# Softmax sums over partitions by accumulating DMAs, values of all groups kept in DRAM, five probability tiles

## The chip, the cores and the metric

The kernel runs on one core of a Trainium2 chip. The metric is the device time of one execution in microseconds. Of each kernel there are several timed runs, whose median counts, and one execution taken with the hardware profiler, whose records are called the trace here. Engines are named as the profile names them: PE is TensorE (matmuls), PEld its weight loads, DVE is VectorE, ACT is ScalarE, POOL is GpSimd, and SP is SyncE, which issues nearly all DMAs. A name such as L364 is line 364 of the kernel before.

## The reference

One input `x` of 2048 tokens by 1024 is normalised and goes two ways.

```
xn  = layernorm(x)
# A: attention, 32 heads of 32
q, k, v = split(xn @ wqkv)
p   = softmax(q @ k.T / sqrt(32), axis=keys)
s   = concat_heads(p @ v) @ wo
# B: a router picks 8 tokens, they go through a SwiGLU FFN (F = 3584) and are added back
r   = xn @ w_r ; idx = top 8 of r
y   = (silu(xn[idx] @ w_gate) * (xn[idx] @ w_up)) @ w_down * sigmoid(r[idx])
g   = silu(xn + scatter(y, idx))
out = x + s * g
```

The change concerns the softmax: each query's exponentials have to be summed over all 2048 keys, and the attention output is divided by that sum. All of it is float32 in and out.

## The kernel before

**Tiling.** The 32 heads are worked on in 8 groups `g` of 4 heads (`NG = 8`, the last is `L = 7`). In a group the 2048 queries are 4 blocks `qb` of 512, and the 2048 keys are 16 tiles `kt` of 128. One step of the main loop is a unit `(g, qb, kt)`; there are 512 units, 16 to a block, 32 blocks in all. Scores are computed with keys on the partitions: for a unit, `scores` makes 4 heads x 128 keys x 512 queries on PE in two halves, and ACT takes the exponential of each half into a probability tile `pt` of 128 x 2048 float32 (L357). No maximum is subtracted. `values` multiplies the tile with the values of its 128 keys (L371) and accumulates over the 16 units in one PSUM bank `oa`.

**The sums.** The denominators need the sum over all keys, thus over units and over partitions. Over units, DVE adds every tile into the tile of `kt = 0` of the block, which is the accumulator (`add`, L364: 15 adds a block). Over partitions, `sums` multiplies the accumulator with a matrix of ones on PE (L389, eight instructions for four heads because float32 takes two each), ACT copies the result (`ds`, L391), and SP writes 4 x 512 numbers to DRAM (`d_d`, L396) and reads them back spread over 128 partitions (`dr`, L397). `reciprocals` takes 1/x on DVE, SP writes it to DRAM and reads it back broadcast to all rows (`rb`, L414), `normalise` multiplies the block's output with it (L420), and `split_o` splits the product in two float16 parts, which SP stores (L429).

**Buffers.** There are four `pt` tiles: one is the accumulator, three rotate. A tile is free again when its add and its value matmuls are done; the accumulator is free after `sums`. Tiles of one tag are given out in the order in which they were freed. `v` has 16 tiles, `hl` two, `o32` (the block's unnormalised output) one.

**Projections.** Beside the units PE computes the next group's Q, K and V (`chain`, `pair_v`, `chain_v`). V is computed for two groups at once for groups 1 to 6 (`pair_v`): the first of the pair goes straight to SBUF, the second to DRAM (`v_d`), from which `load_v` fetches it a group later. Groups 0 and 7 are computed alone (`chain_v`) straight into SBUF.

**Order.** The order on PE, DVE, ACT and SP is written out by hand: a loop runs over the units, and in unit `u` issues `scores(u + 1, 0)`, one item of the filling work, `scores(u + 1, 1)`, `add(u)`, `values(u)`, then what is due in that unit (`side`, filled by `on` and `at`), then more filling work according to its planned cost. A function that returns another one has that one issued a unit later (`go`, `soon`). In each unit's turn of the before kernel, the block before is finished at fixed places:

```python
        if block:
            for at, h in ((1, sums), (5, reciprocals), (9, normalise), (10 if before[0] == L else 11, split_o)):
                if kt == at:
                    go(lambda: h(*before))
```

Every queue works strictly in this order; SP too, so that a DMA that waits for its data holds back all DMAs behind it. GpSimd is not in the hand-written order; it has the router's index work and one gather in group 2, and 16 gathers of the routed rows in the last group. In groups 1 to 3 DVE also runs the router's dot products (`route_dot`), and in blocks 17 to 28 SP fetches the FFN's weights in slices of 448 KB, 96 of them.

## Time and profile before

| | us |
|---|---|
| median of 3 runs | 1687.06 (1686.96 to 1687.82) |
| the profiled execution | 1685.43 |
| span of the profiled execution | 1683.6 |
| PE busy in it | 1651.3 |
| DVE busy | 1420.2 |
| ACT busy | 1195.8 |
| GpSimd busy | 48.0 |
| mean granted TensorE clock | 0.998 |

The span is the time from the first to the last instruction of the program in the trace. A row of a group of instructions reads: line, engine, operation, output<-input, shapes, count | busy us, mean ns of one | idle us of the engine just before them, and what ended it. Matmuls overlap in the array: busy time is the union of their spans, and the time that a group takes from the others is seen from its start to the next group's start. A row of a timeline reads: start us, duration us, engine, line, operation, tiles, count. DMA rows on `SPq` show when SP issued them, not when the data landed. In a stretch's row stand its length, the busy time of each engine with the number of instructions, the granted clock, the DMA engines' busy share and GB/s.

### The profile page before, as it was taken

The page shows a single profiled execution, that of the slowest core. Times are in us where ns is not written, and L with a number is a line of the kernel's source. Part 1 is how long each engine was busy: PE and PEld are TensorE (multiplying, and loading weights), DVE is VectorE, ACT ScalarE, POOL GpSimd, SP SyncE. Part 2 cuts the span into 40 slices and gives each one's busy share as a digit, 9 for nine tenths or more (in the row PEclk, how much of TensorE's full clock was granted, in tenths as well). Part 3 has the DMA queues.
Part 4 walks back from the last instruction along what each step waited for, and adds up shares of the span by engine and source line. Part 5 has one row for each costly group of instructions (what it writes and reads, how often), then busy time and mean ns, then how long its engine had stood idle before and what let it go on. Part 6 is the DMA issues. An engine that isn't in the chain of part 4 may idle for free.

```text
span 1683.6 us, 60567 instructions
## 1 busy us (share of the span) xinstructions
PE 1651.3 (98%) x27809; PEld 951.6 (57%) x27809; DVE 1420.2 (84%) x1122; ACT 1195.8 (71%) x1366; POOL 48.0 (3%) x41
## 2 busy tenths in 40 slices
PE   6999999999999999999999999999999999999998
PEld 5756877756565445455556554444444444455666
DVE  8687788989999989989988888888887989887862
ACT  5666777777787778778777777777777777765530
POOL 0000000000000000000000000000000002021110
PEclk9999999999999999999999999999999999999999
DMA  6222223222332222222334345345434455443442
GB/s 244 82 62 85 68 65 100 66 72 85 109 99 69 68 87 94 74 81 73 95 113 133 114 144 151 104 131 162 132 108 146 120 158 162 133 141 118 158 168 91
DMA packets 129985, 187.98 MB, mean 112 GB/s; under 512 B 21731, under 2 KB 91667, under 8 KB 129467
## 3 DMA queue, kind: packets, MB, share of 16 engines
q1 hardware_dynamic: 127370, 183.86, 35.2%
q8 instruction: 219, 3.59, 0.9%
q0 software_dynamic: 2352, 0.17, 0.1%
q14 instruction: 44, 0.35, 0.1%
HBM read 151.92 MB, written 40.41 MB: 114 GB/s over the span
## 4 chain that ended last, share of the span: by engine, by line
PE 83%; DVE 9%; ACT 3%; issue 3%; DMA 2%; SPq 0%; DVEq 0%; ACTq 0%
PE sc L236 22%; PE oa L371 22%; PE proj L236 16%; PE wop L236 10%; DVE pt L364 6%; PE vp L236 5%; PE vp L276 2%; ACT pt L357 2%; PE dn L389 2%; PE proj L256 2%; PE ffn L565 1%; PE py L596 1%; PE xtp L192 1%; DVE w L226 0%; DVE hl L325 0%
## 5 line engine op out<-in xcount | busy, mean ns | idle before, releaser
L357 ACT ACTIVATE pt<-sc 128x1024 f32<-128x1024 f32 x1024 | 997.4, 1024 | 358.4 <-PE sc L236 274.5
L364 DVE TENSOR_TENSOR pt<-pt 128x2048 f32<-128x2048 f32 x480 | 1097.0, 2288 | 98.1 <-ACT pt L357 80.1
L236 PE MATMUL sc<-qs,ks 96*32 96x512 f16 x8192 | 639.5, 379 | 10.1 <-ACT pt L357 10.0
L371 PE MATMUL oa<-pt,v 128*32 128x512 f32 x4096 | 543.2, 592 | 0.0
L236 PE MATMUL proj<-xt,w 128*32 128x512 f16 x5664 | 428.1, 379 | 0.0
L236 PEld LDWEIGHTS <-ks 96*32 96x32 f16 x8192 | 260.5, 97 | 166.1 <-issue 39.1
L236 PEld LDWEIGHTS <-w 128*32 128x32 f16 x5664 | 184.8, 96 | 216.3 <-issue 138.1
L371 PEld LDWEIGHTS oa<-pt,v 128*32 128x32 f32 x4096 | 149.4, 110 | 80.4 <-ACT o L382 2.8
L236 PEld LDWEIGHTS <-xt 128*32 128x32 f16 x4608 | 145.0, 96 | 80.8 <-issue 64.8
L236 PE MATMUL vp<-w,xt 128*32 128x256 f16 x4608 | 178.2, 272 | 0.0
L236 PE MATMUL wop<-wo,ot 128*32 128x512 f16 (+1 forms) x3168 | 173.5, 373 | 0.5 <-DVE z L708 0.5
L236 PEld LDWEIGHTS <-ot 128*32 128x32 f16 x3168 | 111.2, 97 | 70.8 <-issue 22.0
L325 DVE SCALAR_TENSOR_TENSOR hl<-proj,hl 128x512 f16<-128x512 f32 x64 | 44.1, 689 | 65.8 <-ACT hl L324 65.7
L708 DVE SCALAR_TENSOR_TENSOR z<-wop,z 128x512 f32<-128x512 f32 (+1 forms) x33 | 22.2, 675 | 62.8 <-PE wop L236 62.7
L276 PEld LDWEIGHTS <-xt 128*128 128x128 f16 x768 | 45.5, 100 | 7.7 <-issue 7.2
L276 PE MATMUL vp<-w,xt 128*128 128x128 f16 x768 | 49.2, 223 | 0.0
L324 ACT ACTIVATE hl<-proj 128x512 f16<-128x512 f32 x64 | 38.2, 597 | 14.6 <-PE proj L236 10.6
L565 PEld LDWEIGHTS ffn<-wf,xst 128*32 128x32 f32 x512 | 17.1, 108 | 38.0 <-issue 35.7
L226 DVE SCALAR_TENSOR_TENSOR w<-wraw,w 128x1024 f16<-128x1024 f32 x24 | 29.3, 1220 | 9.1 <-ACT w L221 9.1
L565 PE MATMUL ffn<-wf,xst 128*32 128x224 f32 x512 | 36.3, 352 | 0.0
L192 PE MATMUL xtp<-ident,xin 128*128 128x128 f32 x128 | 19.4, 302 | 15.0 <-DVE xin L183 7.8
L391 ACT ACTIVATE ds<-dn 128x512 f32<-128x512 f32 x32 | 19.2, 599 | 21.1 <-PE dn L389 20.9
(130 smaller groups left out, 636.5 us busy)
## 6 DMA issues: line engine op xcount, KB each, us to landing
st<-hl SPq DMA_DIRECT2D x64, 256.0 KB
wf<-in_B_w_gate_dram SPq DMA_DIRECT2D x32, 448.0 KB
wf<-in_B_w_up_dram SPq DMA_DIRECT2D x32, 448.0 KB
wd<-in_B_w_down_dram SPq DMA_DIRECT2D x32, 448.0 KB
wraw<-in_A_wqkv_dram SPq DMA_DIRECT2D x24, 512.0 KB
ks<-st SPq DMA_DIRECT2D x96, 128.0 KB
qs<-st SPq DMA_DIRECT2D x96, 128.0 KB
xr<-in_A_x_dram SPq DMA_DIRECT2D x16, 512.0 KB
```

Source lines behind the costliest of these rows:

```text
L192: nc.tensor.transpose(XP[t][:, k, :], xn[:, k * P:(k + 1) * P], ident)
L226: nc.vector.scalar_tensor_tensor(hl[:, 1], WR[c, g], WS, hl[:, 0], op0=ALU.mult, op1=ALU.subtract)
L236: nc.tensor.matmul(out[c], w[:, c], x, **flags)
L256: (nc.tensor.matmul if hold is not None else narrow)(box["ps"][:, cols], w[:, wi, k, :], xt[:, xi, k, cols], start=(n == 0), stop=(n == 23))
L276: nc.tensor.matmul(box["ps"][:, tt, :], xt[:, xi, k, t % 4 * P:(t % 4 + 1) * P], w[:, wi, k, :], start=(k + wi + xi == 0), stop=(k + wi == ...
L324: nc.scalar.activation(hl[:, 0], ps, AF.Copy, scale=KQ)
L325: nc.vector.scalar_tensor_tensor(hl[:, 1], ps, KQ, hl[:, 0], op0=ALU.mult, op1=ALU.subtract)
L357: nc.scalar.activation(PT[u][:, 2 * hf:2 * hf + 2], ps, AF.Exp, bias=0.0, scale=ESC)
L364: nc.vector.tensor_add(ACC[g, qb], ACC[g, qb], PT[u])
L371: nc.tensor.matmul(OA[g, qb][32 * j:32 * j + 32, :], VT[g, kt // 2][:, kt % 2, 32 * j:32 * j + 32], PT[u][:, j, :], start=(kt == 0), stop= ...
L389: nc.tensor.matmul(dn[32 * j:32 * j + 32, :], ones, acc[:, j, :], start=True, stop=True)
L565: nc.tensor.matmul(box[i][32 * j:32 * j + 32, :], RT["xst"][:, k, :], wt[:, j * FQ:(j + 1) * FQ], start=(k == 0), stop=(k == KT - 1))
```

## The change

For groups 0 to 6 (28 of the 32 blocks) the sum over partitions no longer goes through PE. `fold` writes the whole accumulator (1 MB) to DRAM from SP, and three DMAs issued by GpSimd add the upper half of its rows to the lower half: rows 64 to 127 onto 0 to 63, then 32, then 16. `fold_load` reads the 16 rows that are left back into SBUF, spread over the partitions (`dr16`), and `fold_rows` adds the 16 on DVE and goes on with the reciprocals as before. The places in the next block move from units 1, 5, 9 and 11 to 1 (`fold`), 9 (`fold_load`), 12 (`fold_rows`), 17 (`normalise`) and 18 (`split_o`); 17 and 18 are units 1 and 2 of the block after. The blocks of the last group keep the matmul with ones and units 1, 5, 9 and 10.

There are five `pt` tiles in place of four and two `o32` in place of one. `v` goes from 16 tiles to 10: the values of groups 1 to 7 are all stored to DRAM, a pair in one copy of ACT and one store, and fetched one by one as the group before ends. Value tiles on their way to DRAM and `ds` share the two `hl` buffers; `dr16` and a router tile share the buffer of `rb`.

```diff
+PTB = 5
...
-    v_d = dram.tile([NG // 2, NT // 2, P, 2, P], F32, name="v_d")
+    v_d = dram.tile([NG // 2, NT // 2, P, 2, 2, P], F32, name="v_d")
...
-    SLOTS = [("pt", 4)] * 8 + [("ks", KSB)] * 4 + [("qs", 2)] * 1 + [("big", 3)] * 1 + [("pt", 4)] * 2
+    SLOTS = [("pt", PTB)] * 8 + [("ks", KSB)] * 4 + [("qs", 2)] * 1 + [("big", 3)] * 1 + [("pt", PTB)] * 2
...
         def out():
-            nc.scalar.activation(v_tile(g, h), box["ps"], AF.Copy, scale=VS)
+            if g == 0:
+                nc.scalar.activation(v_tile(g, h), box["ps"], AF.Copy, scale=VS)
+                return
+            v = sb.tile([P, 2, P], F32, name="vs1", tag="hl", bufs=2)
+            nc.scalar.activation(v, box["ps"], AF.Copy, scale=VS)
+            return lambda: nc.sync.dma_start(v_d[(g - 1) // 2, h, :, :, 0], v)
...
-        VT[g, h] = v = sb.tile([P, 2, P], F32, name="v", tag="v", bufs=16)
+        VT[g, h] = v = sb.tile([P, 2, P], F32, name="v", tag="v", bufs=10)
...
         def out():
-            nc.scalar.activation(v_tile(g, h), box["ps"][:, :, 0], AF.Copy, scale=VS)
-            v = sb.tile([P, 2, P], F32, name="v", tag="v", bufs=16)
-            nc.scalar.activation(v, box["ps"][:, :, 1], AF.Copy, scale=VS)
-            return lambda: nc.sync.dma_start(v_d[g // 2, h], v)
+            v = sb.tile([P, 2, 2, P], F32, name="vs2", tag="hl", bufs=2)
+            nc.scalar.activation(v, box["ps"], AF.Copy, scale=VS)
+            return lambda: nc.sync.dma_start(v_d[(g - 1) // 2, h], v)
...
     def load_v(g, h):
-        nc.sync.dma_start(v_tile(g, h), v_d[(g - 1) // 2, h])
+        nc.sync.dma_start(v_tile(g, h), v_d[(g - 1) // 2, h, :, :, (g - 1) % 2])
...
-            PT[u] = sb.tile([P, 4, 512], F32, name="pt", tag="pt", bufs=4)
+            PT[u] = sb.tile([P, 4, 512], F32, name="pt", tag="pt", bufs=PTB)
...
-        o = sb.tile([P, 512], F32, name="o32", tag="o32", bufs=1)
+        o = sb.tile([P, 512], F32, name="o32", tag="o32", bufs=2)
...
-        ds = sb.tile([P, 512], F32, name="ds", tag="f512", bufs=1)
+        ds = sb.tile([P, 512], F32, name="ds", tag="hl", bufs=2)
...
+    def fold(g, qb):
+        a_d = dram.tile([P, 4 * 512], F32, name="a_d", tag="a_d", bufs=2)
+        nc.sync.dma_start(a_d, ACC.pop((g, qb)).rearrange("p j q -> p (j q)"))
+        for n in (64, 32, 16):
+            nc.gpsimd.dma_start(a_d[0:n], a_d[n:2 * n], accum_op=ALU.add, max_dma_last_dim=4096)
+        DN[g, qb] = a_d
+
+    def fold_load(g, qb):
+        a_d = DN[g, qb]
+        dr = DN[g, qb] = sb.tile([P, 16, 16], F32, name="dr16", tag="rb", bufs=1)
+        nc.sync.dma_start(dr, a_d[0:16].rearrange("r (p q) -> p r q", q=16))
+
+    def fold_rows(g, qb):
+        dr = small.tile([P, 2, 16], F32, name="dr", tag="dr")
+        nc.vector.tensor_reduce(dr[:, 0], DN[g, qb].rearrange("p r q -> p q r"), axis=AX.X, op=ALU.add)
+        DN[g, qb] = dr
+        return reciprocals(g, qb)
...
-        rt = sb.tile([NT, P], F32, name="rt", tag="f512", bufs=1)
+        rt = sb.tile([NT, P], F32, name="rt", tag="rb", bufs=1)
...
-            if qb == 3 and n > 1 and n % 2 == 0:
-                for h in range(7):
-                    on(g, qb, 2 * h + 3, load_v, n, h)
-                on(n, 0, 1, load_v, n, 7)
+            if qb == 3:
+                for h in range(6):
+                    on(g, qb, max(2 * h - 1, h), load_v, n, h)
+                for h in range(6, 8):
+                    on(n, 0, 2 * h - 8, load_v, n, h)
...
+    for b in range(NG * NB):
+        g, qb = divmod(b, NB)
+        for k, f in (((1, sums), (5, reciprocals), (9, normalise), (10, split_o)) if g == L else
+                     ((1, fold), (9, fold_load), (12, fold_rows), (17, normalise), (18, split_o))):
+            if b < NG * NB - 1:
+                at((b + 1) * NT + k, f, g, qb)
...
-        if block:
-            for at, h in ((1, sums), (5, reciprocals), (9, normalise), (10 if before[0] == L else 11, split_o)):
-                if kt == at:
-                    go(lambda: h(*before))
```

More of the change, by code (lines that the diff above doesn't have):

```diff
@@ L925, in _fast @@
         g, qb, kt = u
-        block = g * NB + qb
-        before = divmod(block - 1, NB)
         if kt == 0:
@@ L965, in _fast @@
             sides = sides[1:]
-        for at, h in ((2, sums), (12, reciprocals), (24, normalise), (26, split_o)):
-            if n == at:
+        for k, h in ((2, sums), (12, reciprocals), (24, normalise), (26, split_o)):
+            if n == k:
                 go(lambda: h(L, NB - 1))
```

## The prediction

> **What bounds the kernel now.** I read the page first (shares, then the chain that ended last), then busy times over single blocks, then the groups of instructions, then the timeline around one block's end. A block is 16 units of one query block; the stretches below are cut where a block's first `oa` matmul starts.
>
> ```profile
> PE 1651.3 (98%) x27809; PEld 951.6 (57%) x27809; DVE 1420.2 (84%) x1122; ACT 1195.8 (71%) x1366; POOL 48.0 (3%) x41
> ...
> PE 83%; DVE 9%; ACT 3%; issue 3%; DMA 2%; SPq 0%; DVEq 0%; ACTq 0%
> ```
> ```profile
> core 0: us, PE busy (x) PEld busy (x) DVE busy (x) ACT busy (x) POOL busy (x), PEclk, DMA share, GB/s
> ...
> 459.60:503.79 44.19, 44.19 (x781) 30.36 (x776) 41.21 (x29) 34.42 (x41) 0.00 (x0) 1.00 0.32 98
> 503.79:550.60 46.81, 45.00 (x785) 24.23 (x779) 43.49 (x48) 35.07 (x41) 1.20 (x1) 1.00 0.23 70
> 550.60:599.01 48.41, 45.56 (x789) 23.17 (x785) 46.78 (x44) 35.74 (x41) 0.00 (x0) 1.00 0.24 77
> ...
> 643.22:688.55 45.33, 44.67 (x781) 22.35 (x773) 44.36 (x30) 36.50 (x42) 0.00 (x0) 1.00 0.29 92
> ```
> ```profile
> 1054.89:1100.54 45.65, 45.65 (x702) 21.19 (x698) 39.80 (x25) 34.02 (x39) 0.00 (x0) 1.00 0.45 123
> ```
>
> In an ordinary block TensorE has no gap (44.19 busy of 44.19, so 44.19/16 = 2.76 us a unit) and the granted clock is 1.00. VectorE is second with 41.21, which leaves it 2.98 us. Three blocks of groups 2 and 3 are longer than 44.19, by 2.6, 4.2 and 1.1 us, and there VectorE fills 93 to 98% of the time. So TensorE work that disappears shortens nearly every block, until VectorE's 3 us are used up.
>
> **The removed sums.** Of 32 `dn` groups 28 go.
>
> ```profile
> 418.43 1.08 PE L371 MATMUL oa<-pt,v 128*32 128x512 f32 x8
> ...
> 419.29 1.07 PE L389 MATMUL dn<-pt,ones 128*32 128x512 f32 x8
> ...
> 420.15 0.65 PE L236 MATMUL proj<-xt,w 128*32 128x512 f16 x8
> ```
> ```profile
> L389 PE MATMUL dn<-pt,ones 128*32 128x512 f32 x256 | 33.9, 592 | 0.0
> ...
> L391 ACT ACTIVATE ds<-dn 128x512 f32<-128x512 f32 x32 | 19.2, 599 | 21.1 <-PE dn L389 20.9
> ...
> L312 ACT ACTIVATE v<-vp 128x256 f32<-128x256 f32 x24 | 9.4, 390 | 0.0
> ...
> L229 DVE TENSOR_REDUCE am<-wraw 128x1 f32<-128x1024 f32 x24 | 28.9, 1211 | 0.0
> ...
> L517 DVE TENSOR_REDUCE tf<-eq 128x16 f32<-128x128 f32 x1 | 0.3, 286 | 0.0
> ```
>
> The matmuls overlap, so the 33.9 us of busy time overstates them. From one group's start to the next group's start is 420.15 - 419.29 = 0.86 us, and the group before it is 0.86 us as well, so there is no wait inside. 28 x 0.86 = 24.1 us leave the path. ScalarE loses 28 copies of 0.60 us (16.8) and, with one copy per value pair in place of two at 0.39 each, a little more; it has 10 us free in a block, so this is worth nothing by itself.
>
> **The added reduction.** Each of the 28 blocks gets one `fold_rows` reduction over 256 elements per partition. Between 286 ns for 128 elements and 1211 ns for 1024 a straight line gives 0.42 us; the elements are read with a stride, so the long row's 1.21 us is the upper end. I take 0.42 because the size is near the short row. The reciprocals and the normalisation only move (unit 5 to 12; unit 9 to unit 1 of the block after). VectorE then has 41.6 us in a block of 43.3 us: hidden by what is left of its idle time, 1.7 us; at 1.21 us it would still fit, by 0.9 us.
>
> **The fifth tile.** Where VectorE falls behind, the next exponential has no tile.
>
> ```profile
> ACT pt L357 <- DVE pt L364: 11.2, 9, 2.5
> ```
>
> That is over the two blocks from 503.79 to 599.01 (total, times, longest). One more tile lets VectorE be one unit (2.76 us) later, more than the longest of these waits (2.5), so these blocks should fall to VectorE's own time plus 0.42: 43.9, 47.2 and 44.8 for the three long ones, a gain of 2.9 + 1.2 + 0.5 = 4.6 where three times 0.86 is 2.6. A block cannot beat TensorE's 43.3 plus its few extra transposes, so I take 1.3 of the 2.0 us difference. Bounds: 0 (nothing recovered) and 5.3 (all 7.9 us of the three blocks, less the 2.6 counted).
>
> **The accumulator's tile is held by a store.** In place of the matmul, a 1 MB store on SP's queue now releases it.
>
> ```profile
> 455.99 2.28 DVE L364 TENSOR_TENSOR pt<-pt 128x2048 f32<-128x2048 f32 x1
> ...
> 460.52 9.28 DVE L364 TENSOR_TENSOR pt<-pt 128x2048 f32<-128x2048 f32 x4
> ...
> 495.65 4.68 DVE L364 TENSOR_TENSOR pt<-pt 128x2048 f32<-128x2048 f32 x2
> ```
> ```profile
> 115.24 0.34 SPq L329 DMA_DIRECT2D st<-hl  x1
> 117.54 1.38 SPq L340 DMA_DIRECT2D ks<-st  x3
> ```
> ```profile
> DMA  0000000007999969999000000000000000000000
> GB/s 0 0 0 0 0 0 0 0 0 287 382 410 423 246 205 382 382 396 423 14 0 0 0 0 0 0 0 0 0 0 0 0 0 0 0 0 0 0 0 0
> DMA packets 289, 1.07 MB, mean 89 GB/s; under 512 B 32, under 2 KB 32, under 8 KB 288
> ```
>
> Counting 15 adds to a block, the first of the four at 460.52 is the last one into the old accumulator; it ends at 462.8, 3.2 us into the block (459.60). SP issues the store then; what stands before it is issued by 462.4 (below). Its duration: 256 KB need 2.3 us from issue to the dependent issue (115.24 to 117.54). In the last rows, 1656 to 1668 us in slices of 0.3 us, 1.07 MB pass in about 3.2 us. A 1 MB store is therefore 2.3 + 3.2 x 3/4 = 4.7 us, bounds 4.3 (a start of 1.1 plus the 3.2) and 9.2 (four times the 256 KB trip). It lands 7.9 us into the block. Tiles are handed out in the order in which they were freed; with five, the old accumulator becomes tile 5 of the new block. Its scores go to TensorE in unit 4, about 9.3 us in, and its values start at 13.8; the exponentials take two times 1.02 us, so TensorE waits only if the tile is free later than some 11 us in. Cost nothing; margin 3 us. At the upper end (12.4) the loss is 1.4 us a block.
>
> **The chain of accumulating copies.** No such copy stands in the trace. The nearest rows are GpSimd's gathers.
>
> ```profile
> L647 POOL DMA_INDIRECT up<-y_d,slot_i x16 | 27.3, 1703 | 9.6 <-DMA y_d<-y 5.5 <-POOL up L646 3.5 <-issue 0.6
> ...
> L523 POOL DMA_INDIRECT xs<-in_A_x_dram,sel_i x1 | 1.2, 1203 | 539.0 <-DMA wo_d<-wohl 539.0
> ```
> ```profile
> xs<-in_A_x_dram,sel_i POOLq DMA_INDIRECT x1, 3.2
> ```
> ```profile
> DMA to landing us min/median/max: 2.1/3.5/7.2
> ```
> ```profile
> 461.98 0.38 SPq L320 DMA_DIRECT2D v<-v_d  x1
> 465.36 0.50 SPq L396 DMA_DIRECT2D d_d<-ds  x1
> ...
> 479.91 0.43 SPq L439 DMA_DIRECT2D xr<-in_A_x_dram  x1
> 489.43 0.33 SPq L329 DMA_DIRECT2D st<-hl  x1
> ```
>
> The gather of 128 KB lands 3.2 us after issue. An accumulating copy reads both operands, so I count its bytes twice at 1.07 MB per 3.2 us: 512, 256 and 128 KB add 3.0, 1.5 and 0.8 us to 3.2, in all 14.9 us. Low end 9.6 (three times 3.2), high end 26.9 (three times the longest gather, 7.2, plus 5.3). They depend on each other and run one by one: the last ends 3.2 + 4.7 + 14.9 = 22.8 us into the block (17 to 39 with both ends; past the cover below, that is rival 3). SP waits for the end in `fold_load`; it gets there about when it passed the `xr` load of unit 10, 479.91, 20.3 us in. What it holds back by 2.5 us is queued behind it: that `xr` load, used four units later, and weight slices, issued four units ahead. The next store of projections is at 489.43 (29.8), so the two `hl` buffers are not touched. The load into `dr16` moves 128 KB in 64-byte pieces.
>
> ```profile
> GB/s 0 0 0 0 0 0 0 0 0 0 0 0 0 0 0 0 2 58 50 26 2 0 0 0 0 0 0 51 119 137 222 375 324 358 273 256 222 154 68 154
> ```
>
> Here (476.8 to 479.2, slices of 0.06 us) the 8 KB of `r_d` pass in 64-byte pieces in about 0.25 us, after 477.00; sixteen times that is 4 us, and 2.3 us of trip make 6.3, so `dr16` is there at 29.1. VectorE reaches `fold_rows` behind the add of tile 12, the first of the pair at 495.65: 498.0, 38.4 us in. Cover: 9 us. If it is gone, VectorE stands still, then the exponentials (no tile), then TensorE, microsecond for microsecond, because VectorE has 1.7 us to catch up.
>
> **What else moves.** The values of all groups are loaded (56 loads of 128 KB for 24), each due a few units later. The DMA share is 0.32 in an ordinary block and 0.45 in one with expert weights, so roughly 4 MB more per block, counting reads and writes (90 GB/s), has room. Value stores, output stores and projections now share two `hl` buffers, four or five uses a block at 2.3 us each: nothing. The last two `x` tiles of the start find a free `pt` tile at once; no wait for them is among the costly rows, so nothing. The tail is not touched.
>
> **Sum.** 24.1 + 1.3 = 25.4 us. The profiled execution takes 1685.43 us (span 1683.6, 1.8 around it); 1660.0 after. The median of the runs, 1687.06, lies 1.6 above that execution: 1661.7, so 1662.
>
> **Rivals.**
> 1. VectorE's idle time cannot be used: the 2.98 us are waits for exponentials that come in bursts. Then the twelve blocks of groups 1 to 3 keep their length and add 0.42: 12 x 1.28 = 15 us less gain, 1677. For it: the block at 643.22 has VectorE at 44.36 of 45.33. Against: that same block shows it can run at 98%, and 41.6 of 43.3 is 96%.
> 2. The store is late where expert weights pass (blocks 17 to 28): two slices of 448 KB ahead of it cost 2.8 us and doubled packets time another 3.2, landing at about 12.5 us in, 1.5 us late: 12 x 1.5 = 18 us, 1680.
> 3. Slower: the chain outlasts its cover. It decides once the copies take over 24 us in place of 14.9 (38.4 - 3.2 - 4.7 - 6.3), and turns the sum over once they take 25 (0.9 us late, 28 times). The mechanism would be packets that read, add and write one at a time: 64, 32 and 16 rows of 8 KB in halves are 8, 4 and 2 packets on each of 16 engines, 14 x 2.3 us = 32.2 plus three issues of 1.2. That is 35.8, 11.6 us late in each of 28 blocks: about 1987. For it: nothing shows such a copy. Against: the same engines overlap packets in every row above (1.07 MB in 3.2 us are 16 packets per engine, 0.2 us each).
> 4. GpSimd's issuing blocks the adds. Three issues of 1.7 us a block would put VectorE at 41.2 + 0.4 + 5.1 = 46.7 in twelve blocks, 2.5 over today's 44.2 (+30), and leave some 14 us of gain elsewhere: 1703.
>
> ```profile
> L364 DVE TENSOR_TENSOR pt<-pt 128x2048 f32<-128x2048 f32 x4 | 9.2, 2292 | 1.2 <-ACT pt L357 0.6 <-DVE pt L364 0.5
> ```
>
> This is 1421.5 to 1428.8, with three gathers being issued: 2292 ns each, as everywhere, so no block. The Trainium skill, page "SBUF — State Buffer", section "Who interferes with whom", says that a VectorE instruction with two SBUF inputs contends with a GpSimd instruction that reads SBUF, and the adds are such instructions; by that rule rival 4 would hold if issuing reads SBUF, and the row speaks against it.
> 5. The freed time is lost elsewhere and nothing changes: 1687. Against it stands the missing gap around `dn`.
>
> **Chances.** Forecast 0.58, rival 1 0.12, rival 2 0.10, rival 3 0.09, rival 4 0.05, rival 5 0.06. Faster by over 0.2% (what a measurement here tells from no change) 0.80, within 0.06, slower 0.14. The forecast's own range is 1657 (5.3 us recovered in the long blocks in place of 1.3, and the runs' spread of 0.9) to 1668 (a fifth of the 28 blocks with the store's 1.4 us or the chain's 1 us); with rivals 1 and 2 it is 1655 to 1681, holding 0.80.
>
> **What would show it.** Right: `dn` 32 instructions in place of 256; an ordinary block near 43.3 us with TensorE gapless; `dr16` reductions near 0.42 us with no wait for a DMA before them; copies landing in 3 to 6 us; fewer waits of exponentials for adds. Wrong: idle time of VectorE released by the load of `dr16`, exponentials of tile 5 released by the store, or SP standing in `fold_load` past 30 us into a block.

## The result, and the profile after

The changed kernel takes 1659.34 us (median of 4 runs, 1658.31 to 1661.74) beside 1687.02 of the kernel before (1686.96 to 1687.82): a ratio of 0.9837, 95% interval 0.982 to 0.9854. The forecast was 1662, its own range 1657 to 1668. The profiled execution takes 1658.31 us, with a span of 1656.5 and a mean granted clock of 0.997.

In the code of the changed kernel the lines are a little further down: L237 is the narrow matmuls, L362 the exponential, L369 the add, L376 `oa`, L394 `dn`. New are L410 (the 1 MB store), L412 (the accumulating copies), L418 (the load of `dr16`) and L422 (the reduction in `fold_rows`).

First the page of the changed kernel, busy time by engine:

```profile
PE 1626.2 (98%) x27585; PEld 1067.6 (64%) x27585; DVE 1434.6 (87%) x1150; ACT 1178.8 (71%) x1314; POOL 115.2 (7%) x125
```

TensorE lost 25.1 us of busy time and 224 instructions and is still busy for 98% of a span that is 27.1 us shorter: it is the bound, as before. (The chain of waits breaks off early in this trace, so it isn't used.)

The stretches below are single blocks of the changed kernel: 8 (ordinary), 9 and 10 (with the router's work), 12 (the third of the long blocks before), and 21 (with expert weights). The columns are those of the prediction's stretches.

```profile
453.99:497.34 43.35, 43.35 (x775) 36.80 (x770) 41.86 (x30) 34.36 (x39) 2.40 (x3) 1.00 0.56 152
497.34:541.17 43.83, 43.83 (x776) 26.23 (x772) 42.79 (x49) 34.57 (x40) 3.41 (x4) 1.00 0.46 119
541.17:588.18 47.01, 44.34 (x782) 23.59 (x777) 45.97 (x46) 34.73 (x40) 2.47 (x3) 1.00 0.50 128
631.51:674.79 43.28, 43.28 (x774) 29.28 (x769) 42.92 (x30) 35.94 (x41) 2.39 (x3) 1.00 0.57 150
1034.24:1079.08 44.84, 44.84 (x695) 21.12 (x691) 40.30 (x26) 33.40 (x38) 2.40 (x3) 1.00 0.63 166
```

Block 8 goes from 44.19 to 43.35 us without a gap on TensorE, block 21 from 45.65 to 44.84: one `dn` group each. The three long blocks go from 46.81, 48.41 and 45.33 to 43.83, 47.01 and 43.28, and block 12 runs VectorE for 42.92 of 43.28 us. The DMA share rises from 0.32 to 0.56 in block 8 and from 0.45 to 0.63 in block 21, and TensorE stays gapless in both.

The groups of the changed kernel that answer to the prediction's rows (one row for each shape):

```profile
L369 DVE TENSOR_TENSOR pt<-pt 128x2048 f32<-128x2048 f32 x480 | 1096.7, 2288 | 59.3 <-ACT pt L362 39.9
...
L412 POOL DMA_DIRECT2D a_d<-a_d x84 | 67.8, 808 | 1256.5 <-DMA a_d<-pt 980.9 <-DMA a_d<-a_d 271.3 <-DMA ks<-st 4.2
...
L422 DVE TENSOR_REDUCE dr<-dr 128x16 f32<-128x256 f32 x28 | 16.8, 598 | 0.0
...
L394 PE MATMUL dn<-pt,ones 128*32 128x512 f32 x32 | 4.2, 592 | 0.0
```

`dn` has 32 instructions in place of 256. The reduction takes 598 ns, not 0.42 us, and stands with no idle time before it: no block waits for `dr16`. The adds take 2288 ns with 84 accumulating copies being issued, as they did without.

The fold of one block, in the timelines of SP, GpSimd and VectorE over block 8, which starts at 453.99 (first column: start; in brackets the idle time before and what ended it):

```profile
457.84 0.32 SPq L410 DMA_DIRECT2D a_d<-pt  x1
...
475.93 0.74 SPq L646 DMA_DIRECT2D wo_raw<-in_A_wo_dram  x1
477.52 0.38 SPq L418 DMA_DIRECT2D dr<-a_d  x1
```
```profile
461.98 0.83 POOL L412 DMA_DIRECT2D a_d<-a_d  x1 [30.78 <-DMA a_d<-pt]
468.04 0.79 POOL L412 DMA_DIRECT2D a_d<-a_d  x1 [5.24 <-DMA a_d<-a_d]
473.94 0.78 POOL L412 DMA_DIRECT2D a_d<-a_d  x1 [5.11 <-DMA a_d<-a_d]
```
```profile
490.88 0.60 DVE L422 TENSOR_REDUCE dr<-dr 128x16 f32<-128x256 f32 x1
```

The store is issued 3.9 us into the block and has landed by 8.0, where the first copy starts. The three copies run one by one; SP reaches the load at 477.5, 23.5 us in, when the last has just landed; VectorE reaches the reduction 36.9 us in. Block 8 is one of the quick ones: over the 28 blocks the store takes 4.1 to 11.4 us from its issue to the first copy, which starts 6.9 to 12.6 us into the block, latest in blocks with expert weights (12.3 in block 23, 12.6 in block 28). The landing times over all 28 blocks, from the DMA issues of the changed kernel (KB each, median us from issue to landing):

```profile
a_d<-a_d POOLq DMA_DIRECT2D x28, 512.0 KB, 5.9
...
a_d<-a_d POOLq DMA_DIRECT2D x28, 256.0 KB, 4.6
...
a_d<-a_d POOLq DMA_DIRECT2D x28, 128.0 KB, 3.7
```

And two of the changed kernel's waits (total us, times, longest), the exponentials' for a tile and SP's for the chain:

```profile
ACT pt L362 <- DVE pt L369: 5.5, 8, 1.6
```
```profile
SPq L418 <- DMA a_d<-a_d: 54.7, 18, 6.6
```

Exponentials waited 34.5 us for adds in the whole run before; here it is 5.5, and no exponential waits for the store.

### The profile page after: what moved, and what is told of

Its sections match the earlier page's. It is cut to its first block, busy times and chain, and to the rows that moved or that the text cites. A ratio compares the mean times of both kernels' runs of the same rounds, so it can differ in the third digit from the quotient of the medians.

```text
span 1656.5 us, 60299 instructions
## 1 busy us (share of the span) xinstructions
PE 1626.2 (98%) x27585; PEld 1067.6 (64%) x27585; DVE 1434.6 (87%) x1150; ACT 1178.8 (71%) x1314; POOL 115.2 (7%) x125
## 5 line engine op out<-in xcount | busy, mean ns | idle before, releaser
L362 ACT ACTIVATE pt<-sc 128x1024 f32<-128x1024 f32 x1024 | 997.2, 1024 | 356.6 <-PE sc L237 269.6
L369 DVE TENSOR_TENSOR pt<-pt 128x2048 f32<-128x2048 f32 x480 | 1096.7, 2288 | 59.3 <-ACT pt L362 39.9
L237 PE MATMUL sc<-qs,ks 96*32 96x512 f16 x8192 | 677.4, 380 | 4.2 <-ACT pt L362 4.2
L376 PE MATMUL oa<-pt,v 128*32 128x512 f32 x4096 | 562.2, 593 | 0.0
L237 PE MATMUL proj<-xt,w 128*32 128x512 f16 x5664 | 453.5, 379 | 0.0
L237 PEld LDWEIGHTS <-ks 96*32 96x32 f16 x8192 | 313.8, 97 | 124.0 <-issue 28.6
L237 PEld LDWEIGHTS <-w 128*32 128x32 f16 x5664 | 233.7, 96 | 167.2 <-issue 104.3
L376 PEld LDWEIGHTS oa<-pt,v 128*32 128x32 f32 x4096 | 179.6, 110 | 56.0 <-ACT o L387 2.1
L237 PEld LDWEIGHTS <-xt 128*32 128x32 f16 x4608 | 167.6, 96 | 60.4 <-issue 47.9
L237 PE MATMUL vp<-w,xt 128*32 128x256 f16 x4608 | 190.7, 272 | 0.0
L237 PE MATMUL wop<-wo,ot 128*32 128x512 f16 (+1 forms) x3168 | 173.3, 372 | 0.5 <-DVE z L733 0.5
L237 PEld LDWEIGHTS <-ot 128*32 128x32 f16 x3168 | 108.9, 97 | 73.1 <-issue 22.3
L412 POOL DMA_DIRECT2D a_d<-a_d x84 | 67.8, 808 | 1256.5 <-DMA a_d<-pt 980.9
L330 DVE SCALAR_TENSOR_TENSOR hl<-proj,hl 128x512 f16<-128x512 f32 x64 | 44.1, 689 | 51.3 <-ACT hl L329 50.5
L277 PEld LDWEIGHTS <-xt 128*128 128x128 f16 x768 | 46.2, 101 | 7.7 <-issue 7.2
```

Source lines behind the costliest of these rows:

```text
L237: nc.tensor.matmul(out[c], w[:, c], x, **flags)
L277: nc.tensor.matmul(box["ps"][:, tt, :], xt[:, xi, k, t % 4 * P:(t % 4 + 1) * P], w[:, wi, k, :], start=(k + wi + xi == 0), stop=(k + wi == ...
L330: nc.vector.scalar_tensor_tensor(hl[:, 1], ps, KQ, hl[:, 0], op0=ALU.mult, op1=ALU.subtract)
L362: nc.scalar.activation(PT[u][:, 2 * hf:2 * hf + 2], ps, AF.Exp, bias=0.0, scale=ESC)
L369: nc.vector.tensor_add(ACC[g, qb], ACC[g, qb], PT[u])
L376: nc.tensor.matmul(OA[g, qb][32 * j:32 * j + 32, :], VT[g, kt // 2][:, kt % 2, 32 * j:32 * j + 32], PT[u][:, j, :], start=(kt == 0), stop= ...
```

## The experiments

All experiments start from the changed kernel, but for the last one. Beside medians, each of which is compared with the kernel before on the same chip, the text uses the time of blocks 0 to 9 and 11 to 28, read from one profile per kernel as two stretches; it leaves out the kernel's start, its tail and block 10, whose lengths vary between executions (last section). These are the two stretches of before and after, and their sums are 1288.14 and 1260.90, so 27.2 us were gained there:

```profile
79.15:550.60 471.45, 469.42 (x8558) 305.43 (x8554) 411.00 (x291) 352.88 (x407) 1.20 (x1) 1.00 0.26 81
...
599.00:1415.69 816.69, 811.92 (x13308) 415.76 (x13304) 711.92 (x456) 626.06 (x714) 5.23 (x4) 1.00 0.40 119
```
```profile
80.22:541.17 460.95, 460.95 (x8485) 361.91 (x8481) 413.75 (x297) 346.80 (x385) 22.95 (x28) 1.00 0.47 128
...
588.18:1388.13 799.95, 795.21 (x13164) 476.72 (x13160) 722.94 (x475) 615.77 (x686) 48.65 (x58) 1.00 0.64 174
```

The forecast's theory was: 24.1 us from TensorE's removed sums, a little from the fifth tile, nothing from moving the later steps, and the whole fold hidden.

### Four probability tiles

```diff
-PTB = 5
+PTB = 4
```

> The changed kernel with four probability tiles in place of five; the rest of the change stays. Theory of the prediction (the fifth tile is what lets the 1 MB store hold the accumulator's tile): with four, the old accumulator becomes tile 4 of the next block, whose exponentials are wanted about 6.5 us into the block and without which TensorE stands from about 8.3 us on. In the trace of the changed kernel the first accumulating copy starts 7.6 to 12.6 us into the block, so 0 to 4 us are lost in a block, 27 us in all, and the 4.5 us that the long blocks gained over the removed matmuls go too: 1690, range 1680 to 1700, with exponentials that wait for the store. Rival (the fifth tile only smooths VectorE's bursts): 1664, with the exponentials' new waits on adds.

Measured: 1668.93 us, 0.9887 (0.9872 to 0.9902), about 9.6 us slower than the changed kernel. That is outside the range of 1680 to 1700 and nearer to the rival's 1664. The two stretches are 462.99 and 806.07 us long, 8.2 more in sum. Its waits:

```profile
ACT pt L362 <- DVE pt L369: 44.1, 48, 2.7
...
ACT pt L362 <- DMA a_d<-pt: 9.8, 9, 2.4
```

With four tiles, nine exponentials wait for the store, and the waits for adds go from 5.5 to 44.1 us. So beside the fold the fifth tile is worth 9.6 us. The store's holding a tile costs far less than the 27 us expected for it: nine waits in 28 blocks, none above 2.4 us. How the 8.2 us split between the waits for the store and the far larger ones for adds is not shown.

### The sums back on TensorE, at their old places

```diff
-        for k, f in (((1, sums), (5, reciprocals), (9, normalise), (10, split_o)) if g == L else
-                     ((1, fold), (9, fold_load), (12, fold_rows), (17, normalise), (18, split_o))):
+        for k, f in (((1, sums), (5, reciprocals), (9, normalise), (10 if g == L else 11, split_o))):
```

> The changed kernel with the sums over partitions on TensorE again in all blocks, at units 1, 5, 9 and 11; five tiles and the values in DRAM stay. Theory (28 x 0.86 us of matmuls are the gain, the fifth tile is worth some 4 us): 1659.3 + 24.1 = 1683.4, range 1681 to 1685. Rival (the fifth tile and the stored values carry a good part of the gain by themselves): 1675 or less.

Measured: 1685.52 us, 0.9988 (0.9979 to 0.9998); the kernel before had 1687.31 beside it. Five tiles and all values in DRAM, without the fold and without the moved steps, are worth 1.8 us in the medians, and 2.5 in the stretches:

```profile
80.87:549.87 469.00, 468.86 (x8557) 337.74 (x8553) 408.99 (x286) 352.69 (x395) 0.30 (x1) 1.00 0.28 87
...
599.23:1415.87 816.64, 811.17 (x13308) 421.53 (x13304) 713.91 (x457) 625.63 (x704) 5.23 (x4) 1.00 0.43 126
```

That is near the 1.3 of the forecast, and the median lies just above the expected range of 1681 to 1685. But 24.1 + 1.8 is not 27.7: some 2 us were still without a cause. A part of them stands in TensorE's waits in this kernel:

```profile
PE sc L237 <- ACT pt L362: 4.2, 12, 0.7
PE dn L394 <- DVE pt L369: 3.9, 4, 2.6
```

In the kernel before, TensorE waits 10.0 us for exponentials (the row is in the last experiment) and none of its matmuls waits for an add. With the fifth tile the waits for exponentials are down to 4.2 us, but now the sums, in blocks 10, 11, 12 and 16, wait 3.9 us for VectorE's last add: the tile lets VectorE fall further behind, and `dn` at unit 1 is where TensorE then stands. So the tile's gain is not complete while the sums are on TensorE.

### No sums at all

The store, the copies, the load and the reduction are left out; groups 0 to 6 are divided by a constant, with one `memset` in the reduction's place.

```diff
     def fold(g, qb):
-        a_d = dram.tile([P, 4 * 512], F32, name="a_d", tag="a_d", bufs=2)
-        nc.sync.dma_start(a_d, ACC.pop((g, qb)).rearrange("p j q -> p (j q)"))
-        for n in (64, 32, 16):
-            nc.gpsimd.dma_start(a_d[0:n], a_d[n:2 * n], accum_op=ALU.add, max_dma_last_dim=4096)
-        DN[g, qb] = a_d
+        ACC.pop((g, qb))
...
-        nc.vector.tensor_reduce(dr[:, 0], DN[g, qb].rearrange("p r q -> p q r"), axis=AX.X, op=ALU.add)
+        nc.vector.memset(dr[:, 0], 1.0e9)
```

> The changed kernel without any sum over partitions for groups 0 to 6: no 1 MB store, no accumulating copies, no load of 16 rows, and the reduction of VectorE replaced by a small fill with a constant, so these groups are divided by a constant and not by their sums. Theory (store, copies, load and reduction lie wholly beside TensorE's work): 1659, within 2 us, of which 1 to 2 us less at most in the blocks where VectorE is full. Rival (the 2.0 MB of added transfers per block and the queued store cost time by contention): 1652 or less, with shorter blocks where expert weights pass.

Measured: 1656.76 us, 0.982 (0.9806 to 0.9833). What is left of the fold's price is at most 2 to 3 us, near what the runs can resolve; it was run again below beside the changed kernel.

### The load and the reduction early

```diff
-                     ((1, fold), (9, fold_load), (12, fold_rows), (17, normalise), (18, split_o))):
+                     ((1, fold), (5, fold_load), (6, fold_rows), (17, normalise), (18, split_o))):
```

> The changed kernel with fold_load at unit 5 in place of 9 and fold_rows at unit 6 in place of 12; the copies are the same. Theory (the chain of copies ends 21 to 29 us into the block and the 16 rows some 5 us later, and what hides it is VectorE's place for fold_rows, 36 to 39 us in): at unit 6 VectorE gets there about 19 us in and waits 9 to 12 us in each of 28 blocks; it can catch up 1.5 us in a block of groups 1 to 3 and 5 us in the others, so some 8 us x 12 + 5 us x 16 = 180 us are lost: 1840, range 1760 to 1900, with VectorE's idle time ended by the load of the 16 rows. Rival (the tiles let VectorE stand without TensorE noticing, or the chain is not in the way): under 1690.

Measured: 1787.88 us, 1.0612 (1.0591 to 1.0633), thus 128.5 us slower than the changed kernel. Its group for the reduction:

```profile
L422 DVE TENSOR_REDUCE dr<-dr 128x16 f32<-128x256 f32 x28 | 16.7, 597 | 191.9 <-DMA dr<-a_d 191.9
```

All 28 blocks wait, 6.9 us each in the mean. That is less than the 9 to 12 expected, mostly because VectorE starts on the rows 3.1 to 5.1 us after the load's issue (median 3.4) where the forecast had 6.3. So VectorE's wait does go through to the end: of 191.9 us waited 128.5 are lost. Where the other third goes was not taken apart; and some of the loss is clock (its mean granted clock is 0.977, last section). The chain has a price; in the changed kernel its cover hides it.

### The reduction two units earlier

```diff
-                     ((1, fold), (9, fold_load), (12, fold_rows), (17, normalise), (18, split_o))):
+                     ((1, fold), (9, fold_load), (10, fold_rows), (17, normalise), (18, split_o))):
```

> The changed kernel with fold_rows at unit 10 in place of 12, fold_load still at 9. With fold_rows at unit 6 the 16 rows were there 3.2 to 3.5 us after the load's issue, which makes the ready time 24.5 to 28 us into an ordinary block and up to 32 where expert weights pass. Theory (there is a cover that only has to be long enough; at unit 10 VectorE arrives 29 to 32 us in): no wait in ordinary blocks, some 1 us in a few others that VectorE takes back: 1659, range 1658 to 1662. Rival (every unit by which fold_rows comes earlier costs, as 128 us for six units would suggest, 21 us a unit): 1680 or more.

Measured: 1670.13 us, 0.9889 (0.9874 to 0.9904). By the forecast's cover of 9 us, two units (5.4 us) should have cost nothing; about 10 us were lost, and in few places. VectorE waits for the rows in seven blocks, from 0.2 to 4.6 us; the 3.6 us in block 23 cost nothing. Two rows of VectorE's timeline, the waits in blocks 9 and 27, and the two blocks (497.34 and 1304.39 were their starts in the changed kernel, where they took 43.83 and 40.67 us):

```profile
536.40 0.60 DVE L422 TENSOR_REDUCE dr<-dr 128x16 f32<-128x256 f32 x1 [4.61 <-DMA dr<-a_d]
...
1345.26 0.60 DVE L422 TENSOR_REDUCE dr<-dr 128x16 f32<-128x256 f32 x1 [4.23 <-DMA dr<-a_d]
```
```profile
498.17:546.29 48.12, 45.54 (x776) 26.39 (x772) 42.19 (x46) 34.63 (x40) 2.91 (x4) 0.96 0.42 112
1312.24:1360.04 47.80, 42.83 (x602) 19.45 (x600) 40.57 (x26) 33.67 (x37) 2.62 (x3) 0.93 0.70 188
```

These two blocks lose 4.3 and 7.1 us, block 10 another 2.4 and block 18 0.3; 24 of the 28 keep their length. In block 9 it isn't the chain that is late. SP, in the changed kernel's timeline, issues the load there at 531.84, 34.5 us into the block:

```profile
527.85 0.24 SPq L515 DMA_DIRECT2D pk_d<-pk  x1
...
531.84 0.40 SPq L418 DMA_DIRECT2D dr<-a_d  x1
```

`pk_d` is the router's index store, and SP stands 7.8 us in it for VectorE. So in the router's block the cover is about 1 us in the changed kernel, not 9: queue order, not DMA time, sets it there. In block 27 it is the chain: the first copy starts 11.4 us in, the three land 8.1, 6.3 and 3.3 us after their issue, and SP issues the load right behind, 30.0 us in. The block pays a wait of 4.23 us, then a gap of 4.77 us on TensorE, and then a lower clock (0.93; 0.96 in block 9; last section).

### TensorE's gap in block 10

```diff
-    on(2, 2, 6, routed_turn)
+    on(2, 2, 9, routed_turn)
```

> The changed kernel with the router's transpose (routed_turn) at unit 9 of block (2, 2) in place of 6. In the trace of the changed kernel TensorE stands there for 2.67 us until VectorE has the eight tokens normalised, which is the one gap left in groups 1 to 3. Theory (the fifth tile takes VectorE's bursts, and what is left in this block is this one order of work): the block goes from 47.0 to some 45.7, VectorE's own time in it, or 44.5, so 1 to 2.5 us less: 1657.5. Rival (VectorE is behind in this block anyway and TensorE waits elsewhere for as long): 1659.

Measured: 1660.18 us, 0.9832 (0.9819 to 0.9846), no difference from the changed kernel. The one gap above 1.5 us that TensorE has in the changed kernel's blocks 0 to 28 (2.67 us, before the routed tokens are transposed in block 10) is gone, and block 10 goes from 47.0 to 46.2 us, but blocks 11 and 28 lengthen by about 1 us each.

### The sums on TensorE, with the later steps at the new places

```diff
-                     ((1, fold), (9, fold_load), (12, fold_rows), (17, normalise), (18, split_o))):
+                     ((1, sums), (12, reciprocals), (17, normalise), (18, split_o))):
```

> The kernel with the sums on TensorE (1685.5 measured) with the later steps at the places of the changed kernel: reciprocals at unit 12, normalise at unit 17 and split_o at 18, for groups 0 to 6. The changed kernel is 26.2 us below the one with the sums on TensorE, where the removed matmuls alone are 24.1. Theory (the other 2 us are the moved steps, which take VectorE's work out of the second half of the router's blocks, where it is behind): 1683.4, with shorter blocks 9 to 12. Rival (the moved steps do nothing, the rest is a chain through TensorE that only the missing matmuls shorten): 1685.5.

Measured: 1681.0 us, 0.9963 (0.9949 to 0.9976). Against the same kernel without sums (1656.76, on another chip) it is 24.2 us slower in the medians, and its stretches give 1283.43, 24.2 us above the 1259.27 of that kernel's second run:

```profile
80.97:549.68 468.71, 468.71 (x8559) 346.17 (x8553) 409.80 (x288) 352.04 (x394) 1.20 (x1) 1.00 0.27 86
...
596.06:1410.78 814.72, 810.77 (x13309) 454.65 (x13305) 713.11 (x457) 625.90 (x704) 5.23 (x4) 1.00 0.42 126
```

```profile
PE dn L394 <- DVE pt L369: 1.8, 2, 1.1
```

The removed matmuls are worth close to what the trace of before said, 28 x 0.86 = 24.1. The stretches hold 27 of the 28, thus 23.2; of the 0.9 us above it, 0.7 is the wait of `dn` for an add in block 11 (the other such wait is in block 10). And 1681.0 is 4.5 us faster than 1685.52 with the sums at the old places: moving the reciprocals and the normalisation is not free of effect, it gains. In the stretches it gains 2.2 us (1285.64 to 1283.43); block 10, which they leave out, goes from 49.4 to 46.4 us, but the profile with the old places has a window at half clock there (last section).

### The changed kernel again

> The changed kernel once more, as the reference for the three beside it. Both theories: 1659.3, range 1658 to 1662, the spread that it had.

Measured: 1661.01 us (1659.36 to 1662.94), 0.9851 (0.9836 to 0.9866). It is the base for the next two, and its profile shows a block 10 of 48.67 us (last section).

### One row read in place of sixteen

The reduction on VectorE reads one of the 16 rows; 15 are left out of the sum.

```diff
-        nc.vector.tensor_reduce(dr[:, 0], DN[g, qb].rearrange("p r q -> p q r"), axis=AX.X, op=ALU.add)
+        nc.vector.tensor_scalar(dr[:, 0], DN[g, qb][:, 0], 1.0e4, None, op0=ALU.mult)
```

> The changed kernel with fold_rows reading one of the 16 rows and scaling it, in place of adding all 16: the store, the three copies and the load stay, 15 rows of the sum are left out, and VectorE loses the 0.60 us reduction for a small operation. Without any sum the kernel took 1656.8, 2.6 less. Theory (the 2.6 us are VectorE's reduction, in the blocks where VectorE is full): 1657. Rival (they are the DMAs: the store, the copies, the queue): as the changed kernel, 1659.

The result stands beside that of the next kernel, below.

### No sums, again

> The kernel without any sum over partitions for groups 0 to 6, divided by a constant, once more beside the changed kernel. Theory (store, copies, load and reduction cost 2.6 us together): 2 to 3 us below the changed kernel on the same chip. Rival (the difference was the start, which varies from run to run by 1 to 2 us): within 1 us of it.

Measured: 1658.33 us (0.9833, 0.982 to 0.9847) with one row, 1657.35 (0.9826, 0.9812 to 0.9839) with no sums, beside 1661.01. The intervals overlap, so the stretches decide; these are with one row, and with no sums:

```profile
80.25:541.20 460.95, 460.95 (x8487) 361.94 (x8481) 410.92 (x297) 346.61 (x385) 22.98 (x28) 1.00 0.48 128
...
589.42:1387.83 798.41, 794.99 (x13164) 384.82 (x13160) 713.81 (x474) 616.03 (x686) 48.74 (x58) 1.00 0.65 175
```
```profile
80.54:541.43 460.89, 460.89 (x8487) 308.15 (x8481) 410.45 (x297) 346.54 (x385) 1.20 (x1) 1.00 0.28 87
...
587.88:1386.26 798.38, 795.09 (x13164) 502.77 (x13160) 714.51 (x475) 615.71 (x686) 5.23 (x4) 1.00 0.42 128
```

Their sums are 1259.36 and 1259.27, beside 1260.90. The store, the copies and the load cost about 0.1 us, less than these profiles can resolve, although they raise the DMA share from 0.42 to 0.65; the reduction itself costs 1.5 us, all of it in the second stretch (799.95 against 798.41) and nearly all in blocks 18, 20 and 27, about 0.5 us each. One profile stands behind each of these sums; two profiles of the same kernel differ by 0.2 to 0.3 us. Without the reduction they are 1259.1 and 1259.3 (the two kernels without sums) and 1259.4 (one row), with it 1260.9 and 1260.6 (the changed kernel's two profiles).

### The kernel before, with only the later steps moved

This one starts from the kernel before: four tiles, values as before, sums on TensorE. Only the places are new, with the second `o32` buffer and the router tile in the buffer of `rb` that they need.

```diff
-        o = sb.tile([P, 512], F32, name="o32", tag="o32", bufs=1)
+        o = sb.tile([P, 512], F32, name="o32", tag="o32", bufs=2)
...
-        rt = sb.tile([NT, P], F32, name="rt", tag="f512", bufs=1)
+        rt = sb.tile([NT, P], F32, name="rt", tag="rb", bufs=1)
...
+    for b in range(NG * NB):
+        g, qb = divmod(b, NB)
+        for k, f in (((1, sums), (5, reciprocals), (9, normalise), (10, split_o)) if g == L else
+                     ((1, sums), (12, reciprocals), (17, normalise), (18, split_o))):
+            if b < NG * NB - 1:
+                at((b + 1) * NT + k, f, g, qb)
...
-            for at, h in ((1, sums), (5, reciprocals), (9, normalise), (10 if before[0] == L else 11, split_o)):
-                if kt == at:
-                    go(lambda: h(*before))
```

> The kernel before with one thing changed: reciprocals at unit 12, normalise at 17 and split_o at 18 for groups 0 to 6, with a second o32 buffer and the router's small tile in the buffer of rb, which this needs. Four tiles, sums on TensorE, values as before. With five tiles and the values in DRAM, the move took 1685.5 to 1681.0. Theory (the move takes VectorE's work out of the half block in which it is behind, with or without the fifth tile): 4.5 us below the kernel before, 1682.5. Rival (the move needs the fifth tile): 1687.

Measured: 1680.65 us beside 1686.47 of the kernel before, 0.9965 (0.9952 to 0.9979). Its stretches:

```profile
79.21:548.47 469.26, 468.96 (x8558) 301.04 (x8550) 410.15 (x288) 352.66 (x406) 1.20 (x1) 1.00 0.26 80
...
596.61:1410.69 814.08, 810.85 (x13308) 442.01 (x13308) 711.60 (x456) 626.53 (x714) 5.23 (x4) 1.00 0.40 119
```

469.26 + 814.08 = 1283.34: 4.8 us less than before, from the places alone. With five tiles and all values in DRAM on top (the kernel with sums on TensorE and the later steps at the new places, 1283.43) nothing is added. In the other order the tile and the values come first and give 2.5 us, and the move then gives 2.2: the two remove partly the same waits, so how much belongs to each depends on which is counted first. The waits over the whole run, before and with the places moved:

```profile
DVE pt L364 <- ACT pt L357: 80.1, 92, 4.2
...
ACT pt L357 <- DVE pt L364: 34.5, 34, 2.5
...
PE sc L236 <- ACT pt L357: 10.0, 21, 1.4
```
```profile
DVE pt L364 <- ACT pt L357: 46.8, 51, 4.2
...
ACT pt L357 <- DVE pt L364: 31.6, 32, 2.5
...
PE sc L236 <- ACT pt L357: 7.1, 16, 1.6
```

TensorE's waits for exponentials fall by 2.9 us, the exponentials' for adds by 2.9, and VectorE's adds stand less idle for exponentials (80.1 to 46.8). By the stretches' rows TensorE's gaps shrink from 6.8 to 3.5 us, and its busy time by 1.5. Most of the gain lies in three blocks: 1.5 us in block 9 (46.8 to 45.3), 1.2 in block 12 and 0.6 in block 4; blocks 14, 16 and 27 give about 0.4 each. A reading that fits is that the reciprocals and the normalisation, at units 5 and 9, had put VectorE behind where it could not catch up within the block. That the move gains is shown; which of the moved steps does it, and by which of these waits, is not.

## Why the prediction was right, point by point

**The time** was right, 1659.3 for 1662, and so were the bound and the sign. By stretches, 27.2 us = 24.2 (sums) + 4.8 (moved steps) - 0.1 (tile and values, once the steps are moved) - 1.6 (reduction and DMAs), to rounding. The forecast had 24.1 + 1.3. That it came so near is in part luck: it left out the 4.8 us, gave 1.3 to the tile, and put the reduction's cost at nothing, and these errors partly cancel. Outside the stretches block 10 gained 1.4, the start lost 1.1 (the first block begins at 80.22 in place of 79.15) and the tail, which the change doesn't touch, lost 0.4 (the span's rest after block 28: 268.0 before, 268.4 after); in all the 27.1 us between the spans.

**The removed sums**: 24.1 predicted, 24.2 shown, by the kernel with sums at the new places against the one without any (in the stretches 23.2 of matmuls in 27 blocks, and a wait of 0.7 us that goes with them). The start-to-start distance of 0.86 us was the right price; the busy time (33.9 us for 256 instructions, so 29.7 for 224) would have been 5.6 us too much.

**The added reduction**: 0.42 us predicted, 0.598 measured, inside the stated ends. "Hidden by what is left of its idle time" failed by a little: the 28 reductions are 16.8 us of VectorE, of which 1.5 reach the end.

**"The reciprocals and the normalisation only move"** is the sentence that failed. The step was counted at nothing, and it is the mis-sized term: 5.8 us in the medians and 4.8 in the stretches on the kernel before, 2.2 in the stretches once the tile is there. The trace of before held the hint, VectorE 93 to 98% busy in three blocks, but the prediction put all that could be recovered there on the fifth tile.

**The fifth tile**: 1.3 us predicted. Without the move and the fold it gives about 1.8 together with the values in DRAM; with the move, nothing; with the fold, taking it away costs 9.6. Its size depends on what stands beside it. The mechanism held, TensorE's waits for exponentials fall from 10.0 to 4.2 us; what the prediction did not see is that the sums on TensorE then wait for VectorE (3.9 us), so part of the tile's gain comes only with the removed sums.

**The long blocks** were predicted at 43.9, 47.2 and 44.8 us and took 43.83, 47.01 and 43.28. The first two are right in number, though the reason given (the fifth tile) was at most part of it; block 9 falls to 45.3 us by the move alone.

**The store**: issued 3.2 us into the block and landed at 7.9 by the prediction; 3.9 and 8.0 in block 8, up to 12.6 where expert weights pass. Rival 2's landing at 12.5 so came true in some blocks, and its cost did not: no exponential waited. In block 23 the exponentials of `kt = 5` start 10.9 us in, with the first copy at 12.3, so the held tile is wanted later than the 11 us that the prediction reckoned with. With four tiles some do wait.

**The chain of copies**: 6.2 + 4.7 + 4.0 us predicted, 5.9 + 4.6 + 3.7 measured at landing; in block 8 the last lands 23.4 us in, 22.8 predicted. Counting an accumulating copy's bytes twice, with the gather's 3.2 us as its fixed part, priced an operation that the trace did not hold. Rival 3, packets one at a time, is refuted. The load of `dr16` was priced too high (6.3; a median of 3.4 measured, with the reduction at unit 6), and SP's wait in `fold_load`, 54.7 us in 18 blocks, cost nothing that the stretches show.

**What else moves** (values, their stores, the shared `hl` buffers) was counted at nothing. Together with the fifth tile it makes no difference, 1283.43 with both and 1283.34 without; the two were not taken apart.

**The cover** of 9 us was right for an ordinary block like block 8 (the reduction comes 36.9 us in, the load by about 27) and wrong for the router's block 9, where it is about 1 us, because SP stands in another DMA. In the other blocks it is 4 to 14 us, if the rows come 3.4 us after the load's issue. The prediction looked at SP's queue in an ordinary block alone. It cost nothing, by luck of 1 us.

**Rival 1**, that VectorE's idle time can't be used, is refuted: 42.92 of 43.28 us in block 12. **Rival 4**, GpSimd's issuing blocking the adds: 2288 ns each with 84 copies issued, and 2288 for the 86 adds that overlap an issue. The rule of the Trainium skill (page "SBUF — State Buffer", section "Who interferes with whom") on GpSimd instructions that read SBUF would have made it hold if issuing read SBUF; these copies go from DRAM to DRAM, and issuing them does not slow the adds. **Rival 5**, nothing changes, is refuted by the 27.2 us.

## What to carry to other kernels

Work that is taken from a gapless engine is worth its start-to-start distance, not its busy time. Where a second engine is nearly full and makes the first one wait, a small operation that only moves within the block is a term of its own, to be looked for in these waits and not put at nothing. The busy share alone does not tell: in blocks 5 and 8 VectorE was 93% busy and the move gained nothing, in blocks 14, 16 and 27 it was 91 to 92% busy and 0.4 us were gained. A buffer that removes the same waits is not to be counted again, and it can shift the wait to another instruction, as `dn` shows. A cover has to be read in each kind of block: one block in which another DMA holds the queue, and one in which the chain starts late, decided that the step could not come two units earlier.

## What the hardware showed that was not expected

**A TensorE gap of 2.7 us sometimes halves the clock afterwards, and whether it does hangs on where the gap falls.** In block 10 of the changed kernel TensorE waits 2.67 us for VectorE, in its second profile 2.66. The three stretches of 3.41 us around the gap, first in the profile after, then in the second profile of the same kernel (first number after the stretch: its length; then TensorE's busy time; the clock is the third number from the right):

```profile
556.86:560.27 3.41, 2.04 (x32) 0.66 (x24) 3.03 (x14) 1.94 (x2) 0.39 (x1) 1.00 0.30 56
560.27:563.68 3.41, 2.12 (x36) 1.33 (x40) 3.31 (x6) 0.00 (x0) 0.40 (x1) 1.00 0.66 86
563.68:567.10 3.42, 3.42 (x60) 1.55 (x56) 3.32 (x4) 2.69 (x3) 0.77 (x1) 1.00 0.47 112
```
```profile
555.73:559.15 3.42, 2.81 (x44) 1.11 (x36) 3.18 (x10) 2.52 (x3) 0.00 (x0) 1.00 0.52 101
559.15:562.56 3.41, 1.36 (x24) 1.00 (x28) 3.17 (x10) 0.00 (x0) 0.79 (x1) 1.00 0.55 66
562.56:565.97 3.41, 3.41 (x36) 1.27 (x32) 3.31 (x2) 1.37 (x2) 0.77 (x1) 0.50 0.49 123
```

The clock records change only at multiples of 3.413 us from each other (an execution has its own offset), and the stretches are cut on that grid. In the first the gap falls on both sides of a boundary: TensorE is busy for 2.04 and 2.12 us of the two windows, and the clock stays. In the second it falls in one window, 1.36 of 3.41 busy, and the next window runs at 0.50, with 36 matmuls where the other has 60. That block takes 48.67 us in place of 47.01: 3.41 x 0.5 = 1.7. Over the thirteen profiles of this study, in blocks 0 to 28, 25 windows at full clock were followed by half clock, all with TensorE idle for 1.72 us or more (18 of them in the kernel with the reduction at unit 6); some 5000 were followed by full clock, none with more than 1.86 idle. So from full clock about half a window of idle time decides, within 0.15 us. A window that is already at half clock can be followed by another with less: 0.75 us idle in block 27 of the kernel with the reduction at unit 10. A small change of the schedule can so move a kernel by 1.7 us without any reason of its own. It does not explain by itself why the changed kernel's runs spread over 3.4 us: nine runs of before, taken beside the last four kernels, spread over 3.1 us, and before's profile has no window in these blocks with over 1.5 us idle.

The Trainium skill, page "TensorE: Matmul & The Clock Gate", section "What's actually happening", gives the same half rate, the window of 3413 ns and that it runs freely of the kernel. It puts the throttle after a whole idle window of about 3.4 us; here the traces differ, and they decide: TensorE idle for about half a window is enough.
